# Two layers of cached attention and MLP: weight loads reordered, a fourth K buffer, and the output projection spread over the pair loop

## The chip, the cores and the metric

The kernel runs on one core of a Trainium2 chip. The metric is the device time of one execution in microseconds (us). Engines: PE is TensorE, DVE VectorE, ACT ScalarE, POOL GpSimd, SP SyncE, which here only issues DMAs.

## The reference

Two rounds of the same attention layer and the same MLP, one token for each of eight sequences. `B_w1` and `B_w2` drop out: with a sequence length of one, the shifted groups are all zero.

```python
B, D = 8, 448;  Hq, Hkv, Sk, Dh = 16, 8, 4096, 256;  F = 1792
def A(x, k_cache, v_cache, wq, wo):            # k_cache, v_cache: [B, Hkv, Sk, Dh], bf16
    q = (x @ wq)                               # 16 query heads, two for each K/V head
    p = softmax(q @ k.T * Dh ** -0.5)
    return (p @ v) @ wo
x = x + A(layernorm(x), ...)
x = x + Bmlp(layernorm(x), ...)   # Bmlp(y) = y + gelu(layernorm(y) @ w3) @ w4 at this length
# ... the same two lines once more, with the same caches and weights
```

The work is done in "pairs" of a sequence b and a K/V head h: 64 pairs a layer, 128 in all. A pair needs one K tile and one V tile of 2.10 MB each, and both layers read all of them, so 537 of the 547 MB that the kernel reads are K and V.

## The kernel before

A pair g has three PE steps, in this order: scores S(g), the transposes T(g+1) of the next pair's K, then PV(g). DVE and ACT move the transposes out of PSUM (the memory that PE writes its products to; SBUF, below, is the memory that loads fill), and DVE, POOL and ACT do the softmax meanwhile.

```python
NKT_BANKS = 6      # PSUM banks that take transposed K
KB = 3             # K buffers in SBUF
VB = 2             # V buffers
TB = 1             # buffers for transposed K

def sched_dma_K(g):
    b, h = (g % NPAIR_L) // HKV, (g % NPAIR_L) % HKV      # heads inside, batch outside
    def f(eng, ...):
        if g >= KB:
            wait(eng, S_ktfull, 8 * (g - KB + 1))          # transposes of pair g-KB done
        sig(eng.dma_start(K_nat[g % KB][:, :, :], src), S_k[g % KB], v, 16)
def sched_dma_V(g):
    ...  # waits for PV of pair g-VB

# order of the loads: one queue, in order
sched_dma_misc()                       # x
for g in range(KB): sched_dma_K(g)
sched_dma_wq()
for g in range(VB): sched_dma_V(g)
sched_dma_wo()
sched_dma_K(KB)
sched_dma_w3()
sched_dma_w4()
for g in range(KB + 1, NPAIR):
    sched_dma_K(g)
    sched_dma_V(g - (KB + 1) + VB)     # V runs two pairs behind K
...

def sched_attention_epilogue(gbase):   # after the last pair of a layer
    def pe_part(pe, cp=cp):
        wait(pe, S_oT, 2 * (gbase + NPAIR_L))
        for t_ in range(32):
            hq, c = t_ // 2, t_ % 2
            last = pe.matmul(psA[0:B, 0:D], oT_sb[:, hq, c, 0:B], wo_sb[:, 2 * hq + c, 0:D],
                             start=(t_ == 0), stop=(t_ == 31))
    ...  # DVE: copy, add to x, copy

def sched_q_proj(xnT_ready):           # w3 product of the MLP: the same form, 14 x 4
    for g_ in range(32):
        for kc in range(4):
            kr = P if kc < 3 else 64   # 448 = 3 * 128 + 64
            pe.matmul(psB[:, ...], wq_sb[0:kr, kc, g_ * P:(g_ + 1) * P], xnT_bf[0:kr, kc, 0:B], ...)

def sched_pair(g):                     # [layer norms, softmax, MLP cut]
    sched_scoresT(g); sched_softmax_dve1(g); sched_pool(g); sched_exps(g)
    if g + TB < NPAIR:
        sched_transposes(g + TB); sched_evictions(g + TB)
    sched_reciprocal(g); sched_pv(g); sched_final_mults(g)
```

Between the last pair of layer 0 and the first scores of layer 1 everything depends on everything: projection, three layer norms, the MLP, the q projection. I call this stretch the gap, what follows the last pair of layer 1 the tail, and what precedes the first pairs the head.

Of the kernel before, what the change touches and what calls it, by code (L numbers as in the profile page):

```python
# [5 lines left out]
P = 128  # L6
B = 8
# [7 lines left out]
KTILES = 64  # L15
NPAIR_L = B * HKV
NPAIR = 2 * NPAIR_L
NKT_BANKS = 6
KB = 3
VB = 2  # L20
TB = 1
LN_EPS = 1e-5
INV_SQRT_DH = 1.0 / 16.0
GELU_C = 0.044715
GELU_K2 = 2.0 * math.sqrt(2.0 / math.pi)


def bass_interleave_layers__gqa_block_cached__mixer_s_mlp__decode_kernel(
# [12 lines left out]
):  # L41
    bf = mybir.dt.bfloat16
    f32 = mybir.dt.float32
    ACT = mybir.ActivationFunctionType
    ALU = mybir.AluOpType
    AX = mybir.AxisListType
# [38 lines left out]

    x_bf = nc.alloc_sbuf_tensor("x_bf", [B, D], bf)
    xc_f = nc.alloc_sbuf_tensor("xc_f", [B, D], f32)
    sq_f = nc.alloc_sbuf_tensor("sq_f", [B, D], f32)
    xn_bf = nc.alloc_sbuf_tensor("xn_bf", [B, D], bf)
    ln1_bf = nc.alloc_sbuf_tensor("ln1_bf", [B, D], bf)  # L90
    st_f = nc.alloc_sbuf_tensor("st_f", [B, 8], f32)
    a_bf = nc.alloc_sbuf_tensor("a_bf", [B, D], bf)
    tmp_f = nc.alloc_sbuf_tensor("tmp_f", [B, D], f32)
    xnT_bf = nc.alloc_sbuf_tensor("xnT_bf", [P, 4, B], bf)
    qT_sb = nc.alloc_sbuf_tensor("qT_sb", [P, HQ, 2, B], bf)
# [15 lines left out]
    psK = [nc.alloc_psum_tensor(f"psK{i}", [P, 1024], bf) for i in range(NKT_BANKS)]  # L111
    psS = [nc.alloc_psum_tensor("psA", [P, 512], f32), nc.alloc_psum_tensor("psB", [P, 512], f32)]
    psA, psB = psS
    REG_PV = 64
    REG_Q = 128
    REG_X = 384
# [10 lines left out]
    def pool_consts(gp, c1=c1, c2=c2):  # L127
# [7 lines left out]
                             fill=1.0, base=0, pattern=[[-1, B]], channel_multiplier=1)  # L135
        sig(a, S_pool, c2)
    addop("pool", pool_consts)

    def sched_dma_misc():
        v = S_x.reserve(16)  # L140
# [30 lines left out]
        addop("sync", f)  # L171

    def sched_dma_K(g):
        b, h = (g % NPAIR_L) // HKV, (g % NPAIR_L) % HKV
        v = S_k[g % KB].reserve(16)
        assert v == 16 * (g // KB + 1)
        def f(eng, g=g, b=b, h=h, v=v):
            if g >= KB:
                wait(eng, S_ktfull, 8 * (g - KB + 1))
            src = A_k_cache[b, h].rearrange("(m s) d -> m s d", m=P)  # L180
            sig(eng.dma_start(K_nat[g % KB][:, :, :], src), S_k[g % KB], v, 16)
        addop("sync", f)

    def sched_dma_V(g):
        b, h = (g % NPAIR_L) // HKV, (g % NPAIR_L) % HKV
        v = S_v[g % VB].reserve(16)
        assert v == 16 * (g // VB + 1)
        def f(eng, g=g, b=b, h=h, v=v):
            if g >= VB:
                wait(eng, S_pv, g - VB + 1)  # L190
            src = A_v_cache[b, h].rearrange("(m s) d -> m s d", m=P)
            sig(eng.dma_start(V_nat[g % VB][:, :, :], src), S_v[g % VB], v, 16)
        addop("sync", f)

    def sched_layernorm(src_ap, dst_ap, dve_pre_wait):
        cs = st_f
        c1 = S_dv.reserve(); c2 = S_dv.reserve(); c3 = S_dv.reserve()
        c4 = S_dv.reserve(); c5 = S_dv.reserve()

        def dve_part1(dve, c1=c1, c2=c2, c3=c3, c4=c4, c5=c5):  # L200
            sem, val = dve_pre_wait
            wait(dve, sem, val)
            r = dve.reduce_sum(cs[:, 0:1], src_ap, axis=AX.X)  # L203
            sig(r, S_dv, c1)
            wait(dve, S_dv, c1)
            t = dve.tensor_single_scalar(cs[:, 1:2], cs[:, 0:1], -1.0 / D, ALU.mult)
            sig(t, S_dv, c2)
            wait(dve, S_dv, c2)
            t = dve.tensor_single_scalar(xc_f[:, :], src_ap, cs[:, 1:2], ALU.add)
            sig(t, S_dv, c3)  # L210
            wait(dve, S_dv, c3)
            t = dve.tensor_tensor_reduce(out=sq_f[:, :], in0=xc_f[:, :], in1=xc_f[:, :], scale=1.0,  # L212
                                         scalar=0.0, op0=ALU.mult, op1=ALU.add,
                                         accum_out=cs[:, 2:3])
            sig(t, S_dv, c4)
            wait(dve, S_dv, c4)
            t = dve.tensor_scalar(cs[:, 3:4], cs[:, 2:3], 1.0 / D, LN_EPS, ALU.mult, ALU.add)
            sig(t, S_dv, c5)
        addop("dve", dve_part1)

        a1 = S_ac.reserve(); a2 = S_ac.reserve()

        def act_part(act, c5=c5, a1=a1, a2=a2):
            wait(act, S_dv, c5)
            t = act.activation(cs[:, 4:5], cs[:, 3:4], ACT.Ln)
            sig(t, S_ac, a1)
            wait(act, S_ac, a1)
            t = act.activation(cs[:, 5:6], cs[:, 4:5], ACT.Exp, scale=-0.5)  # L228
            sig(t, S_ac, a2)
        addop("act", act_part)  # L230

        c6 = S_dv.reserve()

        def dve_part2(dve, a2=a2, c6=c6):
            wait(dve, S_ac, a2)
            t = dve.tensor_scalar(dst_ap, xc_f[:, :], cs[:, 5:6], None, ALU.mult)
            sig(t, S_dv, c6)
        addop("dve", dve_part2)
        return c6
# [63 lines left out]
    def ev_done(Fg):  # L303
# [2 lines left out]
            return (S_evd, 6 * gg + dve_fill_idx[ff] + 1)  # L306
        return (S_eva, 2 * gg + act_fill_idx[ff] + 1)

    def sched_transposes(g):
        fill_vals = [S_ktfull.reserve() for _ in range(8)]  # L310
        assert fill_vals[-1] == 8 * (g + 1)
        waits = {}
# [55 lines left out]
    def sched_scoresT(g):  # L368
# [5 lines left out]
        def pe_part(pe, g=g, v_sc=v_sc):  # L374
            cd, ca = pair_evictions_done_counts(g)
            wait(pe, S_evd, cd)
            wait(pe, S_eva, ca)
            wait(pe, S_dv, qT_ready[2 * (g // NPAIR_L)])
            if g >= 2:
                wait(pe, S_oT, 2 * (g - 1))  # L380
            b, h = (g % NPAIR_L) // HKV, (g % NPAIR_L) % HKV
            last = None
            for i in range(NCHUNK):
                for c in range(2):
# [59 lines left out]
    def sched_final_mults(g):  # L444
# [5 lines left out]
        def dv(dve, g=g, vs=vs):  # L450
            wait(dve, S_pv, g + 1)
            wait(dve, S_rec, g + 1)
            b, h = (g % NPAIR_L) // HKV, (g % NPAIR_L) % HKV
            for c in range(2):
                t = dve.tensor_tensor(oT_sb[:, 2 * h:2 * h + 2, c, b],  # L455
                                      ps[:, REG_PV + 2 * c:REG_PV + 2 * c + 2],
# [20 lines left out]
    def sched_pool(g):  # L477
# [11 lines left out]
            sig(t, S_D, v_D)  # L489
        addop("pool", pp)  # L490

    def sched_attention_prologue(layer_idx, x_wait):
        ln_out = sched_layernorm(x_bf[:, :], xn_bf[:, :], x_wait)
        f32_ready = sched_to_f32(xn_bf, ln_out)
        xnT_ready = sched_transpose_T(f32_ready, xnT_bf)
        qT_ready[layer_idx] = sched_q_proj(xnT_ready)

    def sched_attention_epilogue(gbase):
        cp = S_pe.reserve()
        def pe_part(pe, cp=cp):  # L500
            wait(pe, S_oT, 2 * (gbase + NPAIR_L))
            wait(pe, S_wo, 16)
            last = None
            for t_ in range(32):
                hq, c = t_ // 2, t_ % 2
                last = pe.matmul(psA[0:B, 0:D], oT_sb[:, hq, c, 0:B], wo_sb[:, 2 * hq + c, 0:D],  # L506
                                 start=(t_ == 0), stop=(t_ == 31))
            sig(last, S_pe, cp)
        addop("pe", pe_part)
        c1 = S_dv.reserve(); c2 = S_dv.reserve(); c3 = S_dv.reserve()  # L510
        def dv(dve, cp=cp, c1=c1, c2=c2, c3=c3):
            wait(dve, S_pe, cp)
            t = dve.tensor_copy(a_bf[:, :], psA[0:B, 0:D])
            sig(t, S_dv, c1)
            wait(dve, S_dv, c1)
            t = dve.tensor_tensor(tmp_f[:, :], x_bf[:, :], a_bf[:, :], ALU.add)
            sig(t, S_dv, c2)
            wait(dve, S_dv, c2)
            t = dve.tensor_copy(x_bf[:, :], tmp_f[:, :])
            sig(t, S_dv, c3)  # L520
# [3 lines left out]
    def sched_mlp_layer(x_ready):  # L524
# [61 lines left out]
        def pe_y(pe, h_ready=h_vals[3], cpy=cpy):  # L586
# [1 line left out]
            wait(pe, S_dv, h_ready)  # L588
            last = None
            for fc in range(14):  # L590
                last = pe.matmul(psA[0:B, 0:D], hT_bf[:, fc, 0:B], w4_sb[:, fc, 0:D],  # L591
                                 start=(fc == 0), stop=(fc == 13))
            sig(last, S_pe, cpy)
        addop("pe", pe_y)
        r_vals = [S_dv.reserve() for _ in range(5)]
        def dv_res(dve, cpy=cpy, rv=r_vals):
            wait(dve, S_pe, cpy)
            t = dve.tensor_copy(a_bf[:, :], psA[0:B, 0:D])
            sig(t, S_dv, rv[0])
            wait(dve, S_dv, rv[0])  # L600
            t = dve.tensor_tensor(tmp_f[:, :], xn_bf[:, :], a_bf[:, :], ALU.add)
            sig(t, S_dv, rv[1])
            wait(dve, S_dv, rv[1])
            t = dve.tensor_copy(ln1_bf[:, :], tmp_f[:, :])
# [8 lines left out]
        return r_vals[4]  # L613

    sched_dma_misc()
    for g in range(KB):
        sched_dma_K(g)
    sched_dma_wq()
    for g in range(VB):
        sched_dma_V(g)  # L620
    sched_dma_wo()
    sched_dma_K(KB)
    sched_dma_w3()
    sched_dma_w4()
    for g in range(KB + 1, NPAIR):
        sched_dma_K(g)
        sched_dma_V(g - (KB + 1) + VB)
    for g in range(NPAIR - (KB + 1) + VB, NPAIR):
        sched_dma_V(g)

    sched_attention_prologue(0, (S_x, 16))

    for g0 in range(TB):
        sched_transposes(g0)
        sched_evictions(g0)

    def sched_pair(g):
        sched_scoresT(g)
        sched_softmax_dve1(g)
        sched_pool(g)  # L640
        sched_exps(g)
        if g + TB < NPAIR:
            sched_transposes(g + TB)
            sched_evictions(g + TB)
        sched_reciprocal(g)
        sched_pv(g)
        sched_final_mults(g)

    for g in range(0, NPAIR_L):
        sched_pair(g)  # L650
    x_ready = sched_attention_epilogue(0)
    x_ready = sched_mlp_layer(x_ready)
    sched_attention_prologue(2, (S_dv, x_ready))
    for g in range(NPAIR_L, NPAIR):
        sched_pair(g)
    x_ready = sched_attention_epilogue(NPAIR_L)
    x_ready = sched_mlp_layer(x_ready)

    v_out = S_out.reserve(16)
# [59 lines left out]
```

## Time and profile before

| stretch of the profiled execution | from, to (us) | long |
|---|---|---|
| head: start to PV of pair 2 | 0 to 75.2 | 75.2 |
| loop of layer 0: PV of pair 2 to PV of pair 63 | 75.2 to 690.5 | 615.3, 10.09 a pair |
| gap: end of PV 63 to first scores of layer 1 | 692.2 to 743.3 | 51.1 |
| first pairs of layer 1: scores 64 to PV 66 | 743.3 to 771.9 | 28.6 |
| loop of layer 1: PV of pair 66 to PV of pair 125 | 771.9 to 1363.6 | 591.7, 10.03 a pair |
| last two pairs | 1363.6 to 1379.4 | 15.8 |
| tail | 1379.4 to 1417.9 | 38.5 |

The median of the 16 executions taken of it on this occasion was 1416.4 us; the profiled one spans 1417.9 us.

First, lines of the page of the kernel before. The rows of forty are busy tenths, the TensorE clock that the chip granted in tenths of full speed, DMA busy tenths and GB/s, each for 1/40 of the span.

```profile
span 1417.9 us, 53861 instructions
...
PE 1174.8 (83%) x25052; PEld 1138.2 (80%) x25052; DVE 626.0 (44%) x1498; ACT 360.2 (25%) x794; POOL 97.2 (7%) x264
...
PE   1888889998888888888659898878978988888984
...
PEclk9877766687876888777757877788687777777776
DMA  9999999999999999999907999999999999999960
GB/s 359 386 425 425 424 418 420 412 425 424 423 422 419 413 423 415 419 415 422 386 0 306 425 425 426 422 416 412 423 423 410 420 425 424 416 413 416 413 254 0
```

PE is busy for 83% of the span, but DMA is at 9 in every slice of both layers, and only slices 21 and 40 are empty. PE's granted clock is well below full in the loop (0.76, next table).

The stretches of the kernel before, with the busy time of each engine (x instructions), then granted clock, DMA share and GB/s:

```profile
core 0: us, PE busy (x) PEld busy (x) DVE busy (x) ACT busy (x) POOL busy (x), PEclk, DMA share, GB/s
75.20:690.50 615.30, 532.35 (x11714) 524.66 (x11715) 282.84 (x671) 163.58 (x367) 45.91 (x122) 0.76 1.00 420
692.20:743.25 51.05, 26.87 (x239) 17.45 (x239) 16.13 (x47) 7.92 (x12) 0.00 (x0) 0.60 0.27 113
771.90:1363.60 591.70, 517.28 (x11332) 509.82 (x11330) 274.25 (x650) 157.54 (x354) 44.41 (x118) 0.76 1.00 418
1379.40:1417.90 38.50, 18.67 (x106) 9.01 (x106) 12.68 (x36) 4.95 (x8) 0.00 (x0) 0.63 0.00 0
```

In both loops the DMA share is 1.00, at 420 and 418 GB/s. A pair's 4.19 MB take 10.0 us at that rate. PE has 532 us of work in 615 us of loop: it is the second busiest, not far off. In the gap and the tail the DMA share falls to 0.27 and 0.

The timeline of the gap of the kernel before, PE only (start, duration, line, what, in brackets the idle time and what ended it):

```profile
690.47 1.74 PE L404 MATMUL psB<-pT,Vnat 128*128 128x2 bf16 x64 [1.74 <-DMA Vnat<-in_A_v_cache_dram]
692.54 7.90 PE L506 MATMUL psA<-wo_sb,oT_sb 128*8 128x448 bf16 x32 [0.33 <-DVE oT_sb L455]
...
712.36 4.15 PE L537 MATMUL psB<-xnT_bf,w_sb 128*128 128x8 bf16 x56 [0.43 <-DVE xnT_bf L268]
720.12 4.36 PE L591 MATMUL psA<-w_sb,hT_bf 128*8 128x448 bf16 x14 [3.61 <-DVE hT_bf L581]
...
733.10 9.43 PE L282 MATMUL psB<-xnT_bf,wq_sb 128*128 128x8 bf16 x128 [0.43 <-DVE xnT_bf L268]
743.25 0.89 PE L386 MATMUL psA<-qT_sb,KTsb 128*128 128x2 bf16 x28 [0.72 <-DVE qT_sb L291]
```

The projection is 32 matmuls in 7.9 us, and the other engines have nothing to do beside it (DVE 0.2 us, ACT and POOL none, from 692.3 to 700.4 us); the q projection takes 9.4 us. The waits of PE in the kernel before (total us, times, longest):

```profile
PE psK L330 <- issue: 58.8, 37, 3.1
PE psA L386 <- issue: 39.4, 18, 3.2
PE psB L386 <- issue: 34.7, 20, 3.4
...
PE psA L404 <- DMA Vnat<-in_A_v_cache_dram: 17.2, 15, 2.3
PE psB L404 <- DMA Vnat<-in_A_v_cache_dram: 12.6, 11, 2.6
```

"issue" is the largest entry, 133 us over all of PE. Each of the 58 such waits of over 1 us ended 1.2 to 1.6 us after a 16 KB packet of the instruction queue had landed. That queue brought 197 packets, all of 16 KB.

### The profile page before, as it was taken

The page shows a single profiled execution, that of the slowest core. Times are in us where ns is not written, and L with a number is a line of the kernel's source. Part 1 is how long each engine was busy: PE and PEld are TensorE (multiplying, and loading weights), DVE is VectorE, ACT ScalarE, POOL GpSimd, SP SyncE. Part 2 cuts the span into 40 slices and gives each one's busy share as a digit, 9 for nine tenths or more (in the row PEclk, how much of TensorE's full clock was granted, in tenths as well). Part 3 has the DMA queues.
Part 4 walks back from the last instruction along what each step waited for, and adds up shares of the span by engine and source line. Part 5 has one row for each costly group of instructions (what it writes and reads, how often), then busy time and mean ns, then how long its engine had stood idle before and what let it go on. Part 6 is the DMA issues. An engine that isn't in the chain of part 4 may idle for free.

```text
span 1417.9 us, 53861 instructions
## 1 busy us (share of the span) xinstructions
PE 1174.8 (83%) x25052; PEld 1138.2 (80%) x25052; DVE 626.0 (44%) x1498; ACT 360.2 (25%) x794; POOL 97.2 (7%) x264
## 2 busy tenths in 40 slices
PE   1888889998888888888659898878978988888984
PEld 1888889998888787788549898878978988888982
DVE  0444444454444444444424444444444444444443
ACT  0222222232222222222212222222222222222221
POOL 0000000000000000000000000000000000000000
PEclk9877766687876888777757877788687777777776
DMA  9999999999999999999907999999999999999960
GB/s 359 386 425 425 424 418 420 412 425 424 423 422 419 413 423 415 419 415 422 386 0 306 425 425 426 422 416 412 423 423 410 420 425 424 416 413 416 413 254 0
DMA packets 44062, 550.89 MB, mean 389 GB/s; under 512 B 4272, under 2 KB 10176, under 8 KB 10624
## 3 DMA queue, kind: packets, MB, share of 16 engines
q1 hardware_dynamic: 43840, 547.45, 92.6%
q8 instruction: 197, 3.23, 0.9%
q14 instruction: 25, 0.20, 0.0%
HBM read 547.43 MB, written 0.01 MB: 386 GB/s over the span
## 4 chain that ended last, share of the span: by engine, by line
PE 56%; DMA 34%; issue 7%; DVE 3%; ACT 1%; SPq 0%; POOL 0%
DMA Vnat<-in_A_v_cache_dram 32%; PE psK L330 30%; PE psA L404 6%; PE psB L404 6%; PE psB L386 5%; PE psA L386 5%; DMA wq_sb<-in_A_wq_dram 2%; PE psB L282 1%; PE psA L506 1%; PE psA L591 1%; PE psB L537 1%; DVE KTsb L349 0%; ACT L228 0%; DVE st_f L203 0%; DVE sq_f L212 0%
## 5 line engine op out<-in xcount | busy, mean ns | idle before, releaser
L330 PE MATMUL psK<-ident_bf,Knat 128*128 128x128 bf16 x8192 | 703.3, 268 | 61.5 <-issue 58.8
L330 PEld LDWEIGHTS psK<-ident_bf,Knat 128*128 128x128 bf16 x8192 | 674.6, 125 | 73.3 <-issue 70.2
L349 DVE COPY KTsb<-psK 128x1024 bf16<-128x1024 bf16 x768 | 508.0, 688 | 182.3 <-PE psK L330 167.2
L359 ACT COPY KTsb<-psK 128x1024 bf16<-128x1024 bf16 x256 | 259.1, 1012 | 454.6 <-PE psK L330 454.6
L386 PE MATMUL psA<-qT_sb,KTsb 128*128 128x2 bf16 x4096 | 120.7, 165 | 41.4 <-issue 39.4
L386 PE MATMUL psB<-qT_sb,KTsb 128*128 128x2 bf16 x4096 | 121.0, 165 | 34.8 <-issue 34.7
L386 PEld LDWEIGHTS psA<-qT_sb,KTsb 128*128 128x128 bf16 x4096 | 115.2, 98 | 42.9 <-issue 41.6
L386 PEld LDWEIGHTS psB<-qT_sb,KTsb 128*128 128x128 bf16 x4096 | 115.3, 98 | 33.3 <-issue 33.3
L404 PE MATMUL psA<-pT,Vnat 128*128 128x2 bf16 x4096 | 112.6, 163 | 17.4 <-DMA Vnat<-in_A_v_cache_dram 17.2
L404 PEld LDWEIGHTS psA<-pT,Vnat 128*128 128x128 bf16 x4096 | 110.0, 96 | 19.8 <-issue 19.5
L404 PE MATMUL psB<-pT,Vnat 128*128 128x2 bf16 x4096 | 112.7, 163 | 14.5 <-DMA Vnat<-in_A_v_cache_dram 12.6
L485 POOL PARTITION_ALL_REDUCE gm<-pm x128 | 45.4, 355 | 1144.8 <-DVE pm L419 1144.8
L404 PEld LDWEIGHTS psB<-pT,Vnat 128*128 128x128 bf16 x4096 | 110.0, 96 | 16.5 <-issue 14.6
L472 ACT ACTIVATE pT<-psA,nb 128x32 bf16<-128x32 f32 x128 | 36.2, 293 | 271.3 <-DVE nb L429 271.3
L472 ACT ACTIVATE pT<-psB,nb 128x32 bf16<-128x32 f32 x128 | 36.3, 294 | 262.4 <-DVE nb L429 262.4
L419 DVE TENSOR_REDUCE pm<-psA 128x2 f32<-128x64 f32 x64 | 14.4, 225 | 138.1 <-PE psA L386 138.1
L419 DVE TENSOR_REDUCE pm<-psB 128x2 f32<-128x64 f32 x64 | 14.4, 225 | 132.0 <-PE psB L386 132.0
L488 POOL PARTITION_ALL_REDUCE Db<-rs x128 | 51.0, 398 | 124.7 <-ACT pT L472 124.7
L455 DVE TENSOR_TENSOR oT_sb<-psA,rc 128x2 bf16<-128x2 f32 x128 | 14.9, 162 | 93.3 <-PE psA L404 93.3
L455 DVE TENSOR_TENSOR oT_sb<-psB,rc 128x2 bf16<-128x2 f32 x128 | 14.9, 162 | 85.7 <-PE psB L404 85.7
L429 DVE TENSOR_SCALAR nb<-gm 128x2 f32<-128x2 f32 x128 | 21.7, 169 | 61.6 <-POOL gm L485 61.6
L258 PE MATMUL psB<-ident_f,tmp_f 8*128 8x8 f32 (+1 forms) x16 | 2.1, 235 | 41.8 <-DVE tmp_f L245 29.6
(57 smaller groups left out, 210.7 us busy)
## 6 DMA issues: line engine op xcount, KB each, us to landing
Knat<-in_A_k_cache_dram SPq DMA_DIRECT2D x128, 2048.0 KB, 13.7
Vnat<-in_A_v_cache_dram SPq DMA_DIRECT2D x128, 2048.0 KB, 17.1
wo_sb<-in_A_wo_dram SPq DMA_DIRECT2D x1, 3584.0 KB, 44.2
wq_sb<-in_A_wq_dram SPq DMA_DIRECT2D x3, 1024.0 KB, 20.6
w_sb<-in_B_w_dram SPq DMA_DIRECT2D x1, 1568.0 KB, 17.1
w_sb<-in_B_w_dram SPq DMA_DIRECT2D x3, 448.0 KB, 10.6
wq_sb<-in_A_wq_dram SPq DMA_DIRECT2D x1, 512.0 KB, 26.2
w_sb<-in_B_w_dram SPq DMA_DIRECT2D x1, 224.0 KB, 13.7
```

Source lines behind the costliest of these rows:

```text
L282: last = pe.matmul(psB[:, REG_Q + g_ * B:REG_Q + (g_ + 1) * B], wq_sb[0:kr, kc, g_ * P:(g_ + 1) * P], xnT_bf[0:kr, kc, 0:B], start=(kc == ...
L330: last = pe.transpose(psK[slot][:, j * P:(j + 1) * P], K_nat[g % KB][:, i, c * P:(c + 1) * P], ident_bf[:, :])
L349: t = dve.tensor_copy(dst, src)
L359: t = act.copy(dst, src)
L386: last = pe.matmul(ps[:, 2 * i:2 * i + 2], KT_sb[g % TB][:, 2 * i + c, :], rhs, start=(c == 0), stop=(c == 1))
L404: last = pe.matmul(ps[:, REG_PV + 2 * c:REG_PV + 2 * c + 2], V_nat[g % VB][:, i, c * P:(c + 1) * P], pT_sb[par][:, i, :], start=(i == 0), ...
L419: t = dve.tensor_reduce(pm_sb[par][:, :], ps[:, 0:2 * NCHUNK].rearrange("p (i j) -> p j i", j=2), axis=AX.X, op=ALU.max)
L429: t = dve.tensor_single_scalar(nb_sb[par][:, :], gm_sb[par][:, :], -INV_SQRT_DH, ALU.mult)
L455: t = dve.tensor_tensor(oT_sb[:, 2 * h:2 * h + 2, c, b], ps[:, REG_PV + 2 * c:REG_PV + 2 * c + 2], rc_sb[par][:, :], ALU.mult)
L472: t = act.activation(outv, inv, ACT.Exp, bias=nb_sb[par][:, j:j + 1], scale=INV_SQRT_DH, accum_out=rs_sb[par][:, j:j + 1])
L485: t = gp.partition_all_reduce(gm_sb[par][:, :], pm_sb[par][:, :], P, ReduceOp.max)
L488: t = gp.partition_all_reduce(Db_sb[par][:, :], rs_sb[par][:, :], P, ReduceOp.add)
```

## The change

Its intent is to take work out of the serial stretches and to keep loads off the stream where it is full:

1. The pairs run with heads outside and batch inside. So the projection of a head can run as soon as its eight pairs are done: four matmuls, two pairs after the head's last (after pairs 9, 17, ... 57 of a layer, counted from 0), accumulated in a PSUM bank of their own (psY2). Only the last head's four stay after the loop.
2. That bank is taken from the transposes (six to five).
3. A fourth K buffer: 16 KB in each partition of SBUF. Two small buffers are given up, which frees 2.7 KB of that.
4. wq is loaded right behind K of pair 0; w3 and w4 behind V of pair 63, at the end of layer 0.

```diff
-NKT_BANKS = 6
-KB = 3
+NKT_BANKS = 5
+KB = 4
+    def pair_bh(g):
+        layer_local = g % NPAIR_L
+        h = layer_local // B
+        b = layer_local % B
+        return b, h
+    def sched_wo_group(layer, head, half, after_pair, at_epilogue=False):
+        def pe_part(pe, cp=cp):
+            wait(pe, S_wo, 16)
+            wait(pe, S_oT, ...)                   # [cut]
+            for hq in (2 * head, 2 * head + 1):
+                for c in range(2):
+                    pe_last = pe.matmul(psY2[0:B, 0:D], oT_sb[:, hq, c, 0:B], wo_sb[:, 2 * hq + c, 0:D],
+                                        start=(first and k == 0), stop=(lastflag and k == 3))
     sched_dma_misc()
-    for g in range(KB):
+    sched_dma_K(0)
+    sched_dma_wq()
+    sched_dma_K(1)
+    sched_dma_V(0)
+    sched_dma_K(2)
+    sched_dma_V(1)
+    sched_dma_wo()
+    for g in range(3, KB):
         sched_dma_K(g)
-    sched_dma_wq()
-    [V0, V1, wo, K3, w3, w4]
+    for g in range(KB, NPAIR):
+        sched_dma_K(g)
+        sched_dma_V(g - KB + VB)
+        if g - KB + VB == NPAIR_L - 1:
+            sched_dma_w3()
+            sched_dma_w4()
     [in sched_pair]
+            for head in range(HKV):
+                if lp == head * B + B + 1:
+                    wo_counts.append(sched_wo_group(layer, head, 0, g))
```

The rest of the diff renames buffers (ln1_bf for a_bf, tmp_f for sq_f) and adds two names that nothing uses.

## The prediction

> **What bounds it now.** The forty-slice table shows the DMA engines at 9 tenths or more throughout both attention layers. Cut into stretches, the trace has DMA share 1.00 to 1.01 and 419 GB/s from 46 to 692 us, and 0.97 from 743 to 1379 us. Each of 128 pairs moves 2 x 2.10 MB, 10.0 us at 419 GB/s; measured, a pair takes 10.03 us. PE is nearly co-critical: T (64 transposes) 5.5 us mean, scores 1.9, PV 1.8, and about 1 us of idle that the waits call "issue" (133 us in all, each just after a 16 KB instruction packet landed[...]). PE waits for V only 30 us in total. Outside the stream lie the head (PE waits 18 us for wq; q projection ends at 40 us), the gap between layers (692.3 to 743.2 us) and the tail (1379.4 to 1417.9 us); in the last two DMA is mostly idle and the chain is serial.
>
> **What the change does.**
> 1. Output projection: 28 of 32 matmuls move into the pair loop. The timeline shows the 32 taking 7.9 us in the gap and 9.1 us in the tail. Four at the cold clock take 1.5 us. Saves 6.4 and 7.5 us. The seven groups cost PE about 7 us a layer inside the loop, where PE has little slack; I charge 3 us a layer.
> 2. w3 and w4 leave the head of the stream and queue behind V of pair 63, loading while DMA would idle. From packet times they occupy the stream about 9 us (448 packets of 3584 B at 141 ns and 1792 of 896 B at 41 ns, over 16 engines); all later loads of layer 0 come 9 to 10 us earlier. They land before the MLP needs them.
> 3. wq moves ahead of K1 and K2: q projection starts near 20.5 instead of 30.7 us. Alone worth nothing where the stream binds, but PE must start earlier to profit from item 2.
> 4. A fourth K buffer: one more K (4.9 us of stream) loads in the gap, but the stream restarts 1.6 us later (at PV of pair 64, not at the transposes of 65): about 3 us. In the loop K already lands 10 to 16 us before use; V order and gating don't change. Small gain.
> 5. Five transpose banks instead of six: the sixth fill waits for the first eviction. At warm clock it starts 2.3 us after T begins; that eviction ends about 1.7 us after. Nearly free.
> 6. Head-outer pair order: same bytes, other addresses; neutral.
>
> **Sum.** -9.5 (w3, w4) -6.4 (gap) -7.5 (tail) -3 (K) +6 (projection in loop) = -20.4 us.
>
> Predicted 1396 us; 8 in 10 between 1384 and 1409. Faster by over 2% (below 1388.6): 0.22; within 2%: 0.76; slower: 0.02.
>
> **Right if** last PV to the projection's copy shrinks to about 1.5 us at both ends; PV of pair 2 comes near 65 us, not 75; the gap is near 44.5 us; the pair period stays 9.9 to 10.1 us at DMA share 1.0; waits for DVE before transposes stay under 10 us.
>
> **Wrong if** PE sets the period: then the loop lengthens by all 14 us of moved matmuls and about 1403 remains. Or the deeper K queue prevents stalls and the period falls to 9.87 us (425 GB/s), giving some 15 us more. Or five banks stall warm transposes, or the new addresses change packet time (611 ns now).

## The result, and the profile after

The changed kernel takes 1389.49 us (median of 8, 1388.72 to 1391.52) against 1416.4 us: 26.9 us less. The ratio is 0.9811, 95% interval 0.9800 to 0.9821: 1.9% faster, so "within 2%", to which the prediction gave 0.76. Ratios here are the mean time of one kernel's fast runs over that of the other's in the same rounds, so they are not quite the ratio of the medians quoted.

Where the time came from, in the two traces:

| stretch | before | after | difference | summed |
|---|---|---|---|---|
| head, to PV of pair 2 | 75.2 | 64.8 | -10.4 | -10.4 |
| loop of layer 0 | 615.3 | 615.6 | +0.3 | -10.1 |
| gap (with PV 63) | 52.8 | 45.6 | -7.2 | -17.3 |
| scores 64 to PV 66 | 28.6 | 23.0 | -5.6 | -22.9 |
| loop of layer 1 | 591.7 | 591.7 | 0.0 | -22.9 |
| last two pairs | 15.8 | 15.5 | -0.3 | -23.2 |
| tail | 38.5 | 30.9 | -7.6 | -30.8 |

The two profiled executions are 30.8 us apart and the medians 26.9: the profiled one before was the slowest of its 16 (1419.65 us). So a row is good to 2 or 3 us. The page of the changed kernel, the same lines:

```profile
span 1387.1 us, 53875 instructions
...
PE 1173.3 (85%) x25052; PEld 1139.9 (82%) x25052; DVE 628.5 (45%) x1498; ACT 360.2 (26%) x794; POOL 97.2 (7%) x264
...
PE   4898798889888888889669998889889889778993
...
PEclk9667867786777888776758678777787777888675
DMA  9999999999999999999947999999999999999970
GB/s 366 414 424 426 424 425 426 424 423 425 415 414 421 420 423 415 425 419 407 384 200 315 425 426 423 425 425 425 411 425 425 422 411 423 425 416 419 413 311 1
```

The stretches of the changed kernel, columns as before:

```profile
64.80:680.40 615.60, 541.22 (x11742) 530.45 (x11743) 284.07 (x669) 161.87 (x365) 45.89 (x122) 0.76 1.00 420
682.10:726.00 43.90, 19.67 (x210) 14.60 (x210) 16.14 (x47) 8.69 (x13) 0.00 (x0) 0.58 0.63 258
749.00:1340.70 591.70, 522.27 (x11359) 511.66 (x11357) 275.94 (x651) 157.55 (x354) 44.39 (x118) 0.77 1.00 419
1356.20:1387.10 30.90, 10.96 (x79) 6.07 (x78) 12.69 (x36) 4.95 (x8) 0.00 (x0) 0.56 0.00 0
```

Both loops are as long as before, to 0.3 us, though PE now has 9 and 5 us more busy time in them. DMA share is still 1.00. In the gap DMA now works for 0.63 of the time: the rest of w3 and w4 (their packets run from 670.8 to 687.8 us) and one more K load come there. The timeline of the gap, PE only:

```profile
680.35 1.75 PE L416 MATMUL psB<-pT,Vnat 128*128 128x2 bf16 x64
682.51 0.92 PE L523 MATMUL psY<-wo_sb,oT_sb 128*8 128x448 bf16 x4 [0.42 <-DVE oT_sb L467]
...
695.35 4.15 PE L566 MATMUL psB<-xnT_bf,w_sb 128*128 128x8 bf16 x56 [0.43 <-DVE xnT_bf L276]
703.12 4.15 PE L620 MATMUL psY<-w_sb,hT_bf 128*8 128x448 bf16 x14 [3.62 <-DVE hT_bf L610]
...
715.89 9.43 PE L290 MATMUL psB<-xnT_bf,wq_sb 128*128 128x8 bf16 x128 [0.43 <-DVE xnT_bf L276]
726.04 1.85 PE L398 MATMUL psA<-qT_sb,KTsb 128*128 128x2 bf16 x64 [0.72 <-DVE qT_sb L299]
```

The projection is down to 0.9 us; the other pieces are as long as they were, to 0.2 us. The waits of PE in the changed kernel:

```profile
PE psK L342 <- issue: 56.0, 37, 3.0
PE psA L398 <- issue: 41.1, 20, 3.2
PE psB L398 <- issue: 33.2, 19, 3.2
...
PE psA L416 <- DMA Vnat<-in_A_v_cache_dram: 6.9, 6, 2.7
PE psK L342 <- DVE KTsb L361: 4.0, 6, 0.9
```

The waits for V fell from 29.8 to 9.6 us in all (the last 2.7 us are those before L416 psB on the page). This suggested two explanations of the equal loops.

**Theory A.** The DMA stream sets the pace of the loops. PE has room; the projection matmuls in the loop are free, and what counts is bytes taken off the stream and serial time.

**Theory B.** PE sets the pace or is even with the stream. The moved matmuls did cost about 14 us, and the fourth K buffer paid for them by removing 20 us of waits for V.

### The profile page after: what moved, and what is told of

It reads as the page before. It is cut to its first block, busy times and chain, and to the rows that moved or that the text cites. A ratio compares the mean times of both kernels' runs of the same rounds, so it can differ in the third digit from the quotient of the medians.

```text
span 1387.1 us, 53875 instructions
## 1 busy us (share of the span) xinstructions
PE 1173.3 (85%) x25052; PEld 1139.9 (82%) x25052; DVE 628.5 (45%) x1498; ACT 360.2 (26%) x794; POOL 97.2 (7%) x264
## 4 chain that ended last, share of the span: by engine, by line
PE 70%; DMA 14%; issue 9%; SPq 3%; DVE 3%; ACT 1%; POOL 0%; ACTq 0%
PE psK L342 40%; DMA Vnat<-in_A_v_cache_dram 14%; PE psB L416 7%; PE psA L416 7%; PE psB L398 7%; PE psA L398 7%; SPq L189 3%; PE psY L523 1%; PE psB L290 1%; PE psY L620 1%; PE psB L566 1%; ACT L236 0%; DVE KTsb L361 0%; DVE st_f L211 0%; DVE tmp_f L220 0%
## 5 line engine op out<-in xcount | busy, mean ns | idle before, releaser
L342 PE MATMUL psK<-ident_bf,Knat 128*128 128x128 bf16 x8192 | 705.4, 269 | 61.5 <-issue 56.0
L416 PE MATMUL psA<-pT,Vnat 128*128 128x2 bf16 x4096 | 112.8, 163 | 8.5 <-DMA Vnat<-in_A_v_cache_dram 6.9
L416 PEld LDWEIGHTS psA<-pT,Vnat 128*128 128x128 bf16 x4096 | 110.0, 96 | 9.7 <-issue 9.6
L416 PE MATMUL psB<-pT,Vnat 128*128 128x2 bf16 x4096 | 112.3, 163 | 4.7 <-DMA Vnat<-in_A_v_cache_dram 2.7
L416 PEld LDWEIGHTS psB<-pT,Vnat 128*128 128x128 bf16 x4096 | 109.8, 96 | 6.0 <-issue 4.2
L441 DVE TENSOR_SCALAR nb<-gm 128x2 f32<-128x2 f32 x128 | 21.7, 169 | 61.5 <-POOL gm L497 61.5
## 6 DMA issues: line engine op xcount, KB each, us to landing
w_sb<-in_B_w_dram SPq DMA_DIRECT2D x3, 448.0 KB, 13.5
wq_sb<-in_A_wq_dram SPq DMA_DIRECT2D x1, 512.0 KB, 16.4
```

Of the source, the lines that this page charges most:

```text
L342: last = pe.transpose(psK[slot][:, j * P:(j + 1) * P], K_nat[g % KB][:, i, c * P:(c + 1) * P], ident_bf[:, :])
L416: last = pe.matmul(ps[:, REG_PV + 2 * c:REG_PV + 2 * c + 2], V_nat[g % VB][:, i, c * P:(c + 1) * P], pT_sb[par][:, i, :], start=(i == 0), ...
L441: t = dve.tensor_single_scalar(nb_sb[par][:, :], gm_sb[par][:, :], -INV_SQRT_DH, ALU.mult)
```

## The experiments

Each kernel ran beside the kernel before on the same chip; kernels of one session shared those runs. Experiments 1 to 4 are one session; 5, 6, 7 and 11 a second; 8, 9, 10 and 12 a third. All but one compute the result as it should be.

### 1. The projection back after the loop

```diff
-                if lp == head * B + B + 1:
+                if False and lp == head * B + B + 1:
...                                     # and all eight heads scheduled after the last pair
```

> The changed kernel with all 32 output-projection matmuls of a layer put back after the last pair (still into psY2). Theory A, the stream sets the pace and PE has room: the matmuls in the loop cost nothing, so taking them out of it gains nothing and only the serial part comes back, 7.1 us in the gap and 7.6 us in the tail, about 14.5 us: near 1404 us. Theory B, PE sets the pace and the fourth K buffer paid for the matmuls by removing waits for V (29 us before, 9.5 us after): the loops shorten by the 14 us of PE time that the matmuls add (8.9 and 5.0 us of PE busy time in the two loops), so the total stays within 3 us of 1389.5. The charge in the prediction (6 us of 14) would give 1397 to 1398.

Measured: 1403.09 us, ratio 0.9906 (0.9892 to 0.9919). Against the changed kernel's 0.9811 that is 13 us slower, as theory A has it. The loop of layer 1 runs at 10.01 us a pair, against 10.03 with the matmuls in it. Taking them out of the loop gained nothing there.

### 2. Eight unused matmuls with each group

```diff
+            if not at_epilogue:
+                for r in range(8):
+                    hq, c = 2 * head + (r % 4) // 2, r % 2
+                    pe.matmul(psS[(after_pair + 1) % 2][0:B, 128:512], oT_sb[:, hq, c, 0:B],
+                              wo_sb[:, 2 * hq + c, 0:384], start=True, stop=True)
```

> The changed kernel with eight more matmuls of 384 columns after each of the seven groups of a layer, into columns of the score bank that nobody reads: 112 more, by the mean spacing of the four real ones (0.23 us for 448 columns) about 1.6 us a group, 22 us of PE time in all; results stay right. Theory A: at most 3 us slower than the changed kernel, 1389 to 1393. Theory B: most of it shows, 1405 to 1412. The charge in the prediction (43% of added PE time) would give 1399.

Measured: 1389.75 us, ratio 0.9823 (0.9808 to 0.9838): no difference from the changed kernel that these intervals show. The prediction's charge is out, and theory B as it stands. That PE sets the pace and hides the work by running faster, this run alone doesn't exclude. How PE took the work is in its groups of instructions. First the transposes of the changed kernel, then the transposes and the added matmuls of this one (name, shapes, count, busy us, mean ns, idle before):

```profile
L342 PE MATMUL psK<-ident_bf,Knat 128*128 128x128 bf16 x8192 | 705.4, 269 | 61.5 <-issue 56.0
```

```profile
L342 PE MATMUL psK<-ident_bf,Knat 128*128 128x128 bf16 x8192 | 685.2, 264 | 58.8 <-issue 51.8 <-DVE KTsb L361 6.6
...
L532 PE MATMUL psA<-wo_sb,oT_sb 128*8 128x384 bf16 x112 | 21.7, 340 | 0.0
```

The added matmuls took 21.7 us, and the 8192 transposes took 20.2 us less. Experiments 5 and 10 look closer at that.

### 3. Three K buffers

```diff
-KB = 4
+KB = 3
...                                     # the order of the loads kept, V two pairs behind K
```

> The changed kernel with three K buffers, all else kept (five banks, order of loads, V two pairs behind K). Theory A: only the K that is loaded in the gap is lost, 4.9 us of stream less the 1.6 us earlier restart: 3 to 4 us slower, 1393. Theory B: waits of PE for V come back to about 30 us and show: 1400 to 1409.

Measured: 1394.54 us, ratio 0.9844 (0.9830 to 0.9857): 4 to 5 us slower than the changed kernel. That is theory A's size. PE waited 16.4 us for V (11.5 and 4.9), 7 us more than in the changed kernel, but the loop of layer 1 stayed at 10.04 us a pair: here a wait of PE in the loop was not time of the kernel while the stream was full (DMA share 1.00).

### 4. w3 and w4 in the head again

```diff
     for g in range(3, KB):
         sched_dma_K(g)
+    sched_dma_w3()
+    sched_dma_w4()
...
-        if g - KB + VB == NPAIR_L - 1:
-            sched_dma_w3()
-            sched_dma_w4()
```

> The changed kernel with w3 and w4 loaded in the head again, behind wo and K3. Theory A: their 9 to 10 us of stream come back in full, 1399. Theory B: PE sets the pace, so a later stream is caught up within the first layer by PE's slack or not needed: 1389 to 1393.

Measured: 1400.06 us, ratio 0.9883 (0.9870 to 0.9897): 10 us slower. Theory A. The timeline of this kernel around PV of pair 2, PE only, shows where the bytes are waited for:

```profile
59.70 3.29 PE L342 MATMUL psK<-ident_bf,Knat 128*128 128x128 bf16 x36
74.57 1.85 PE L416 MATMUL psA<-pT,Vnat 128*128 128x2 bf16 x64 [11.58 <-DMA Vnat<-in_A_v_cache_dram]
```

PE is early (wq still comes early here) and waits 11.6 us for V of pair 2, which stands behind w3 and w4. PV of pair 2 is at 74.6 us, as late as in the kernel before.

### 5. Half of each load

```diff
-            sig(eng.dma_start(K_nat[g % KB][:, :, :], src), S_k[g % KB], v, 16)
+            n = NCHUNK if g < 8 else NCHUNK // 2
+            sig(eng.dma_start(K_nat[g % KB][:, 0:n, :], src[:, 0:n, :]), S_k[g % KB], v, 16)
...                                     # the same for V
```

> The changed kernel with only half of every K and V tile loaded from pair 8 on (the other half of each buffer keeps old data, so the result is wrong on purpose); PE, DVE and ACT do the same work. It shows PE's own pace. If PE has room (theory A): with 8.9 us of PE busy time a pair (541 us over 61 pairs in the loop) and shorter instruction stalls the pair falls from 10.03 to 8.5 to 9.4 us, 75 to 180 us less over 120 pairs, and the DMA share falls to about 0.6. If PE sets the pace: the pair stays at 9.8 to 10.0 us.

Measured: 1190.94 us (1183.04 to 1199.87). Its output is wrong, which doesn't matter for the time. The values stayed inside the comparison's tolerance. The loops of this kernel, from pair 8 to 63 and 66 to 125:

```profile
122.70:588.70 466.00, 448.06 (x10592) 441.68 (x10590) 246.79 (x607) 146.99 (x330) 41.51 (x110) 0.86 0.69 258
658.40:1153.40 495.00, 480.38 (x11360) 474.08 (x11358) 265.02 (x650) 157.67 (x354) 44.52 (x118) 0.85 0.67 249
```

A pair now takes 8.47 and 8.39 us, with PE busy for 96 to 97% and DMA at 0.69 and 0.67. So with half the bytes to load, PE does a pair in about 8.4 us, a little less than expected: PE's work by itself does not hold the pair at 10.0 us. But this is not PE's pace beside the full stream. The "issue" waits of PE shrank from about 132 to 34 us with the lighter DMA load (0.76 us a pair), and the granted clock rose from 0.76 to 0.85. Experiment 6 shows PE beside the full stream.

### 6. wq behind K2 again

```diff
-    sched_dma_K(0); sched_dma_wq(); sched_dma_K(1); sched_dma_V(0); sched_dma_K(2); sched_dma_V(1)
+    for g in range(3): sched_dma_K(g)
+    sched_dma_wq()
+    for g in range(VB): sched_dma_V(g)
```

> The changed kernel with wq behind K0, K1 and K2 again. The q projection starts 10 us later, the stream's bytes and order after the first six transfers are the same. If the stream alone sets the pace: 0 to 2 us slower, since PE at about 9 us a pair catches up with a stream at 10 us. If an early PE start is worth something of its own, as the prediction held (PE must start earlier to profit from the shorter head): 5 to 10 us slower.

Measured: 1393.57 us, ratio 0.9840 (0.9827 to 0.9853), about 4 us slower than the changed kernel: between the two expectations. In its trace PV of pair 2 starts at 71.1 us, 6.3 us later than in the changed kernel, and the lag shrinks (3.4 us at pair 8, 2.0 at pair 20). The stretch from PV of pair 2 to PV of pair 8, columns as before:

```profile
71.10:129.50 58.40, 54.23 (x1156) 53.58 (x1154) 28.28 (x67) 16.03 (x36) 4.52 (x12) 0.74 1.00 423
```

PE is late here and waits for no load, so this is its own pace beside the full stream: 9.73 us a pair, and 9.98 from pair 8 to 20. It does catch up, but by a few tenths of a us a pair, not by the 1.6 us that experiment 5 might suggest. What the 4 us of the medians consist of, this run doesn't settle.

### 7. The kernel before with five banks and the new pair order

```diff
-NKT_BANKS = 6
+NKT_BANKS = 5
-    b, h = (g % NPAIR_L) // HKV, (g % NPAIR_L) % HKV
+    b, h = (g % NPAIR_L) % B, (g % NPAIR_L) // B
```

> The kernel before with five transpose banks instead of six and the pair order of the changed kernel (heads outside, batch inside), nothing else. Prediction: both neutral, within 2 us of before. Rival: the other addresses change the packet time, or the transposes wait for evictions in the warm clock: a change over 4 us.

Measured: 1417.33 us, ratio 1.0011 (0.9998 to 1.0024). Together they are neutral; they were not tried one by one.

### 8. The changed kernel once more, as a control

> The changed kernel itself again, on the same chip as the next three: 1389 to 1391 us. All theories agree; it says how far runs of separate sessions may be compared.

Measured: 1391.11 us, ratio 0.9816 (0.9802 to 0.9829). Sessions agree within 2 us, and their ratios better than that, so I compare ratios across sessions.

### 9. The fourth K buffer without the other parts

The edits of experiments 1, 4 and 6 together, on the changed kernel.

> The changed kernel with three of its parts undone together: the projection after the last pair, w3 and w4 in the head, wq behind K2. What is left against before is the fourth K buffer, five banks and the pair order. If the parts add up as they did one by one (13.6, 10.6 and 4.1 us over 1389.5), it takes 1418 us and the fourth buffer gives nothing alone. If the two head parts overlap (both make the first pairs late, and the later of the two hides the other) and the fourth buffer is worth the 3 to 5 us of the single run: 1412 to 1414.

Measured: 1413.98 us, ratio 0.9978 (0.9965 to 0.9992): 3 us faster than the kernel before. The head parts do overlap. Adding the two head parts to this kernel gives the kernel of experiment 1, so the three ratios 0.9978, 0.9906 and 0.9811 split the gain. In us (differences of ratios times 1416, each good to 2 or 3 us):

| part | ratio from, to | worth (us) | in the prediction |
|---|---|---|---|
| fourth K buffer (with five banks and the order) | 1 to 0.9978 | -3.1 | -3 |
| head: wq early, w3 and w4 late | 0.9978 to 0.9906 | -10.2 | -9.5 |
| projection into the loop | 0.9906 to 0.9811 | -13.5 | -13.9, +6 for the loop |
| together | | -26.8 | -20.4 |

One by one, w3 and w4 were worth 10 us and wq 4, but both together only 10. The early wq alone is worth nothing (experiment 4), and late w3 and w4 alone some 6 us (experiment 6 against 4), since a pair starts when both PE and the stream are there.

### 10. Eight unused matmuls after every pair

```diff
+            def extra(pe, g=g):
+                for r in range(8):
+                    pe.matmul(psS[(g + 1) % 2][0:B, 128:512], qT_sb[:, r, 0, 0:B],
+                              wq_sb[:, r % 3, 0:384], start=True, stop=True)
+            addop("pe", extra)
```

> The changed kernel with eight unused 384-column matmuls after every one of the 128 pairs: 1024 of them, 199 us of PE busy time at the 0.194 us each that the 112 took. If added work on PE is only absorbed by its idle time (1.2 us a pair), the pair becomes about 8.9 + 1.55 + 1.0 = 11.4 us and the kernel some 170 us slower. If it also keeps the clock up, so that transposes shorten as much as the added work takes (705 to 685 us when 22 us were added), the pair takes about 8.45 + 1.55 = 10.0 us, the pace of the stream, and the kernel is 0 to 20 us slower.

Measured: 1403.82 us, ratio 0.9905 (0.9888 to 0.9922): 12.7 us slower than the control of the same session, for 211 us of added PE work. The groups of PE in this kernel, then its two loops:

```profile
L342 PE MATMUL psK<-ident_bf,Knat 128*128 128x128 bf16 x8192 | 542.3, 232 | 26.5 <-issue 23.8 <-DVE KTsb L361 2.1
...
L685 PE MATMUL psA<-wq_sb,qT_sb 128*8 128x384 bf16 x512 | 105.7, 355 | 1.5 <-issue 1.5
L685 PE MATMUL psB<-wq_sb,qT_sb 128*8 128x384 bf16 x512 | 105.6, 354 | 0.2 <-issue 0.2
```

```profile
64.80:685.90 621.10, 567.88 (x12227) 496.98 (x12228) 267.58 (x670) 161.88 (x365) 45.91 (x122) 0.92 1.00 418
757.40:1348.10 590.70, 546.35 (x11832) 480.45 (x11830) 259.08 (x650) 157.56 (x354) 44.40 (x118) 0.92 1.00 419
```

The transposes fell from 705.4 to 542.3 us, the "issue" waits from about 132 to 89 us, and the granted clock in the loops rose from 0.76 to 0.92. The loop of layer 1 stays at 10.01 us a pair, and PE waits for no load in it; the loop of layer 0 grew by 5.5 us, to 10.18 a pair. Given this work, PE got faster, nearly up to the pace of the stream. How busy PE is can't be all that sets its clock: here it is busy for 91 to 92% of the loops at a clock of 0.92, in experiment 5 for 96 to 97% at 0.85. Whether it was the amount of the added work, its kind (384 columns at a time) or its place in the pair, no run separates. The clock records of the kernel before are 111 at 0.5 and 111 at 1.0, those of the changed kernel 107 and 107, with no others, so a granted clock between the two is a mean over time. What switches it was not shown.

### 11. One row count in the serial products

```diff
+    def pad_zero(dve, v=S_dv.reserve()):
+        for t in (xnT_bf[64:128, 3, :], w3_sb[64:128, 3, :], wq_sb[64:128, 3, :]):
+            i = dve.memset(t, 0.0)
+        sig(i, S_dv, v)
-                    kr = P if kc < 3 else 64     # q projection and w3 product
+                    kr = P
```

> The changed kernel with the last contraction block of wq, w3 and the transposed activations padded with zeros from 64 to 128 rows, so that all matmuls of the q projection and of the first MLP product have one shape. In the trace of the changed kernel the start-to-start step of the weight loads is about 120 ns into and out of a 64-row load and 15 to 40 ns between 128-row ones. If the shape change costs that, q projection falls from 9.4 to about 4 us and the MLP product from 4.15 to about 1.7 us: 7.8 us in the gap and 2.4 us in the tail, 1379 us; the head gains nothing if the stream sets the pace there. If the step is due to something else (weights from HBM-loaded tiles, the cold clock): no change, 1389.

Measured: 1380.49 us, ratio 0.9750 (0.9737 to 0.9762): 9 us faster than the changed kernel, of 10 expected. The timeline of its gap, PE only:

```profile
697.13 1.64 PE L572 MATMUL psB<-xnT_bf,w_sb 128*128 128x8 bf16 x56 [0.43 <-DVE xnT_bf L282]
...
716.40 3.55 PE L296 MATMUL psB<-xnT_bf,wq_sb 128*128 128x8 bf16 x128 [0.43 <-DVE xnT_bf L282]
```

The w3 product went from 4.15 to 1.64 us and the q projection from 9.43 to 3.55 us, with the same number of matmuls and more rows. The cost came with the 64-row matmuls among the 128-row ones. That it lies in the change and not in 64 rows as such is not shown: every 64-row matmul here stands between two of 128, and a run with the 64-row ones side by side was not made. Nor does a run show the mechanism.

### 12. Fewer vector instructions in the serial parts

On top of experiment 11: the residual additions read PSUM directly and write x at once, and the layer norm ahead of a transpose writes float32 directly.

```diff
-            t = dve.tensor_copy(ln1_bf[:, :], psY2[0:B, 0:D])
-            t = dve.tensor_tensor(tmp_f[:, :], x_bf[:, :], ln1_bf[:, :], ALU.add)
-            t = dve.tensor_copy(x_bf[:, :], tmp_f[:, :])
+            t = dve.tensor_tensor(x_bf[:, :], x_bf[:, :], psY2[0:B, 0:D], ALU.add)
...                                     # likewise after the MLP, and in the layer norms
```

> The padded kernel with fewer vector instructions in the serial parts: both residual additions read PSUM directly and write x without a copy, and the layer norms ahead of a transpose write float32 at once. By the timeline of the changed kernel each gap loses about 1.0 + 1.4 + 0.9 us and the tail 1.0 + 1.4 + 0.5 us. If serial time counts in full: 6 us less than the padded kernel, 1374 to 1376. If something else sets the time there: 1380.

Measured: 1372.81 us, ratio 0.9690 (0.9678 to 0.9703), 7.7 us faster than the padded kernel by medians of two sessions, more than the 6 expected. The gap is down to 32.9 us and the tail to 25.3. This version beats both kernels, by 43 us and 17 to 18 us.

### Not tried on the chip

A layer norm that takes the inverse root by a power on DVE, instead of a logarithm and an exponential on ACT, did not compile.

## Why the prediction was right, and where it was wrong

The time lay in the stated range, 1389.5 in 1384 to 1409, and 6.5 us under the stated 1396. Point by point:

- *What bounds it.* That the stream binds was right: the pair stays at 10.0 us when PE's work is taken out or added (experiments 1, 2 and 10, layer 1) and falls with the bytes (5). "PE is nearly co-critical" was right as a description: beside the full stream PE took 9.7 to 10.0 us a pair with no load to wait for (experiment 6). What it was used for was wrong. Its 8.9 us of busy time and 1 us of "issue" idle a pair were added up as if fixed, so that more work must cost. They are not fixed: PE does a pair in 8.4 us with half the loads, with shorter "issue" waits (34 us against about 132) and a higher clock (0.85 against 0.76, experiment 5), and where it was given more to do, the clock rose to 0.92 and the transposes shortened from 705 to 542 us (experiment 10). How PE comes out at the stream's pace is open: in the layer-1 loop of the changed kernel it waits for V only about 2 of 592 us.
- *Item 1, the projection.* The serial part was right: 7.2 us off the gap and 7.6 us off the tail in the traces, 6.4 and 7.5 predicted. The term that failed is "+6 (projection in loop)", from the step "where PE has little slack; I charge 3 us a layer". Experiments 1 and 2 show no cost in the loop that their intervals (about 2 us) would reveal, and experiment 10 shows 12.7 us for fifteen times the work. Its right size was about 0, and this one term is nearly the whole 6.5 us.
- *Item 2, w3 and w4.* Right: 9.5 predicted, 10 measured. They did land in time.
- *Item 3, wq.* Right in kind: with w3 and w4 in the head, an early wq is worth nothing (PE just waits, experiment 4; its ratio of 0.9883 is that of experiment 9 less the 0.0095 of the projection), and without it the gain of item 2 is 4 us smaller (experiment 6).
- *Item 4, the fourth K buffer.* 3 predicted; 3.1 alone, 4 to 5 when taken out. The mechanism is in the traces: with three buffers (before, experiments 3 and 7) the stream restarts 9.1 to 9.2 us after the first scores of layer 1 and the last load lands 628 to 630 us after them; with four (the changed kernel, its control, experiments 1 and 9) it restarts at 10.6 to 10.7, has one K less to bring, and the last load lands at 623 to 624. The row "scores 64 to PV 66" of the table (28.6 to 23.0 us) is another matter: PE waits for no load there. Its transposes took 17.9 us before and 15.1 after, and 2.8 us of "issue" waits are gone; the other kernels with three buffers, of experiments 3 and 7, take 25.6 us. It did not speed up the loop, as predicted.
- *Items 5 and 6.* Neutral together, as predicted (experiment 7). PE's waits for DVE before transposes were 4.0 us.
- *What would show it right* came but for one: 1.4 us from the last PV's end to the projection's copy in the gap, but 2.1 in the tail, where 1.5 was predicted for both; PV of pair 2 at 64.8 us, "near 65"; a gap of 43.9 us, "near 44.5"; pairs at 10.03 to 10.09 us at a DMA share of 1.00.

## What to carry to other kernels

Before charging for work that is moved onto the second busiest engine, add unused work of that kind to it and measure (experiment 2, one run); its busy time plus idle time is no measure of what more work costs, least of all on PE, whose clock and "issue" waits changed with the load here (0.76 to 0.92 in experiment 10, about 132 to 34 us in experiment 5). Taking load off the busiest engine (experiment 5) showed that the other can go faster (8.4 us a pair), but not how fast it goes beside the full load (9.7 to 10.0, experiment 6). Where a stream sets the pace, as here, three things paid: bytes moved to where the stream idles (10.2 us with the early wq), loads that the stream can take on during a serial stretch (3.1 us), and the serial stretches themselves (13.5 us, and 9 and 7.7 us in experiments 11 and 12). And look at serial products for mixed matmul shapes: here the padding of 64 rows to 128 gave 9 us for a handful of lines.

## Further measurements

- Beside a full DMA stream PE stood about 130 us in "issue" waits, 58 of them over 1 us in the kernel before, each ending 1.2 to 1.6 us after an instruction packet landed. With half the loads it was 34 us (experiment 5). That fetching is the cause was not tested by itself.
- Weight loads of the q projection and the w3 product, in both traces: a single load took 100 ns for 64 rows, 102 to 118 ns for 128. But every step between a load of 64 and one of 128 rows took 116 to 123 ns from start to start, against 15 to 40 ns between two of 128, and without the 64-row loads the q projection and the w3 product ran about 2.6 times as fast (9.43 to 3.55 us and 4.15 to 1.64 us, experiment 11).
- Loads into this one core ran at 418 to 420 GB/s in the loops, in single slices at up to 426.
- Two issues of loads took long here, and held up SP; each stood behind a load of many small pieces. In the changed kernel the issue of K3, behind wo with its 4096 pieces of 896 bytes, took 38 us (the timeline of SP below), and that of K66, behind w4 with 1792 such pieces, 16 us. From 7 to 45 us, meanwhile, the DMA share was 1.01, so the stream lost nothing; why it happens was not tested.

```profile
6.42 0.45 SPq L164 DMA_DIRECT2D wo_sb<-in_A_wo_dram  x1
6.92 38.26 SPq L189 DMA_DIRECT2D Knat<-in_A_k_cache_dram  x1
```
